# Queries and keys laid out dimensions first, and a scheduler that knows kinds of TensorE products

## The chip, the cores and the metric

The kernel runs on one core of a Trainium2 chip. The metric is the device time of one execution in microseconds (us), the median of several. TensorE (PE) multiplies, VectorE (DVE) and ScalarE (ACT) work element by element, SyncE (SP) issues most DMAs. All arithmetic that matters is in fp32 or in pairs of fp32r numbers (a high and a low part).

## The reference, cut to what matters

Attention with a feature map, then a mixture of experts, then a gated layer. Batch 4, 8 heads, 576 positions of 64 dimensions, 128 features.

```python
def phi(x):
    proj = np.einsum('bhsd,df->bhsf', x, w_phi)
    proj = proj - np.max(np.abs(proj), axis=-1, keepdims=True)
    return np.concatenate([np.exp(proj), np.exp(-proj)], axis=-1)
q_p, k_p = (phi(q), phi(k))
kv = np.einsum('bhsf,bhsd->bhfd', k_p, v)
z = np.sum(k_p, axis=2)
num = np.einsum('bhsf,bhfd->bhsd', q_p, kv)
den = np.einsum('bhsf,bhf->bhs', q_p, z)[..., None] + 1e-06
attn = num / den
# x = attn as (2304, 512): each row goes through the expert of its largest gate logit:
#   relu(x @ w1[e]) @ w2[e], times two gates; 8 experts, 1024 hidden
# then rms norm, silu(xn @ w_gate) * (xn @ w_val) @ w_out; 1536 hidden
```

## The kernel before

**Stages.** In the first stage attention and experts of the four batches are interleaved; near its end the weights of the gated layer are decoded from float64. The second stage is the gated layer in five units of rows; it has a scheduler object of its own, in which no kind of product is ever named. Between them stands a conditional for rows whose expert was guessed wrongly (L978).

**Attention, batch by batch.** A batch has nine projections: four of keys (two heads by 512 positions each), one of the leftover 64 positions of all heads, keys and queries together ("L"), four of queries. Each (`proj`, L411) takes a tile `qk` that was loaded with positions on partitions, turns it with four 128x128 transposes (L418) into a bank of the tag `pa`, copies that with ACT to `x0` (L421), and multiplies it with `w_phi` in eight products of 64 rows (L428; one half of the array for each head) into a double bank `pp`. DVE then takes the largest absolute value (L432) and subtracts it (L434), which frees `pp`. Keys: two exponentials on ACT, products with the values into half columns of the array (L492), a sum over positions on DVE (L478 to L484) that is turned by products with ones (L501), a transposition (L539). Queries: transposes (L447, recorded under L210, which calls them), two exponentials, products with 64 output partitions (L589), normalisation on DVE, transposes (L597, under L210 too), then the high part on ACT and the low part on DVE (L602) into `xh`, the experts' input.

**Experts.** `moe` multiplies in chunks of 12 matmuls of 288 columns (L737, L746), which use the whole array. It needs all of its batch's `xh`. There are two tiles `xh` and eight tiles `h` for the hidden rows, so at most two batches are under way.

**Order.** Every operation is a task with an engine, a modelled duration, a rank (`prio`; attention 100 per batch, experts from 1000) and buffers. `emit` walks through modelled time: of each engine's startable tasks it takes the one that can start first, and of those that can start when the engine comes free the one of lowest rank. The order so found is the order of instructions on each engine; on the chip an engine follows it whatever the times are. Tasks of TensorE go through `products`, which can weave tasks of kinds "load" and "pass" together. No task has the kind "load", so `products` takes one task at a time, as the other engines do. What it costs TensorE to go from whole-array products to products on half the rows or half the columns stands in the tasks' durations: 0.2 us added to each projection and to L589, 0.1 us to L492 and L501.

**Banks.** `pa` has four banks and `pp` two double ones. After a number of releases one `pp` and one `pa` go over to the experts' tag `ph` (L314, L315).

Of the kernel before, what the change touches and what calls it, by code (L numbers as in the profile page):

```python
# [41 lines left out]
class Graph:  # L42
# [4 lines left out]
    def __init__(self):  # L47
        self.free = {e: 0.0 for e in ("PE", "ACT", "DVE", "POOL", "SP")}
        self.cand = {e: [] for e in self.free}
        self.slots, self.log, self.leaving = {}, [], {}  # L50
        self.dma, self.now, self.open, self.tasks = 0.0, 0.0, 0, []
# [29 lines left out]
    def t(self, eng, dur, fn, r=(), w=(), rw=(), use=(), prio=0, nbytes=0, kind=None, steps=1, at=0.0):  # L81
        k = Task()
        k.kind, k.steps = kind, steps
        k.eng, k.dur, k.fn, k.prio, k.nbytes = eng, dur, fn, prio, nbytes
        deps = set()
        for b in r:
            deps.update(b.writers)
        for b in rw:
            deps.update(b.all)
        k.bufs = list(dict.fromkeys(list(r) + list(w) + list(rw) + list(use)))  # L90
        for b in k.bufs:
            b.all.append(k)
            b.left += 1
        for b in list(w) + list(rw):
            b.writers.append(k)
        k.n, k.succ, k.ready, k.end, k.seq = 0, [], at, None, len(self.tasks)
        for d in deps:
            if d.end is not None:
                k.ready = max(k.ready, d.end + self.lat(d.eng, eng))
            else:  # L100
                d.succ.append(k)
                k.n += 1
        self.tasks.append(k)
        self.open += 1
        if k.n == 0:
            self.cand[eng].append(k)
        return k
# [14 lines left out]
    def emit(self, until=()):  # L122
        until = list(until)
        while self.open:
            if until:
                while until and until[-1].end is not None:
                    until.pop()
                if not until:
                    break
            best = None  # L130
            for e, f in self.free.items():
                pick = None
                for k in self.cand[e]:
                    s = self.start(k)
                    if s is not None:
                        key = (max(s, f), k.prio, k.seq)
                        if pick is None or key < pick[0]:
                            pick = (key, k)
                if pick and (best is None or pick[0][0] < best[0][0]):
                    best = pick  # L140
            assert best is not None, "no task can start"
            s, k = best[0][0], best[1]
            if k.eng == "PE":
                self.products(s, k)
            else:
                self.take(k)
                k.fn()
                self.done(k, s, s + k.dur)
# [30 lines left out]
    def products(self, s, k):  # L179


        def ready(kind, wait=0.02):
            w = [(self.start(q), q) for q in self.cand["PE"] if q.kind == kind]
            return sorted((q for t, q in w if t is not None and t <= s + wait), key=lambda q: (q.prio, q.seq))

        if k.kind == "pass" and not ready("load") and ready("load", HOLD):
            rest = [q for q in ready(None) if q.prio >= 1000]
            if rest:
                k = rest[0]
        self.take(k)  # L190
        group = [k]
        n = {"load": 0, "pass": 0, k.kind: k.steps}
        while k.kind:
            short = "pass" if n["pass"] < n["load"] else "load"
            more = ready(short)
            if not more or len(group) > 1 and short == "load":
                break
            self.take(more[0])
            group.append(more[0])
            n[short] += more[0].steps  # L200
        todo = []
        for kind in ("load", "pass"):
            todo.append([(q, i + 1, f) for q in group if (q.kind or "pass") == kind
                         for i, f in enumerate(q.fn() if q.kind else [q.fn])])
        at, ends = s, []
        for i in range(max(map(len, todo))):
            for seq in todo:
                if i < len(seq):
                    q, n, f = seq[i]
                    f()  # L210
                    at += q.dur / q.steps
                    if n == q.steps:
                        ends.append((q, at))
            if i < min(map(len, todo)):
                at -= 0.05
        for q, end in ends:
            self.done(q, s, end)
        self.free["PE"] = at

# [9 lines left out]
class K:  # L229
    def __init__(self, tc, q, k, v, w_phi, wg, wo, w1, w2, mg, mv, mo, rg, out):  # L230
        self.tc, self.nc = tc, tc.nc
        self.q, self.k, self.v, self.w_phi = q, k, v, w_phi
# [69 lines left out]
    def psum(self):  # L302
# [12 lines left out]
        self.g.retire("pa", 36, one[3], "ph", lambda: one[3:])  # L315
# [35 lines left out]
    def attn_slots(self, ctx):  # L351
# [3 lines left out]
        mk("qk", 4, [P, 2, NC, D])  # L355
        mk("v", 3, [P, 2, NC, D])
        mk("vl", 2, [P, 2, NC, D])
        mk("x0", 2, [P, NC, P])
# [17 lines left out]
    def attn(self, b, prio):  # L376
# [6 lines left out]
        def load(src, pr, np_):  # L383
            t = g.buf("qk")
            if pr != "L":
                g.t("SP", 0.5, lambda: nc.sync.dma_start(
                    t.ap, src[b, 2 * pr:2 * pr + 2, 0:MAIN].rearrange("h (p c) d -> p h c d", c=NC)),
                    w=[t], prio=np_, nbytes=2 * MAIN * D * 4)
                return t
            for i, m in enumerate((self.k, self.q)):  # L390
                for j in range(2):
                    g.t(eng, 0.6, lambda i=i, j=j, m=m: dma(
                        t.ap[j * 64:(j + 1) * 64, i], m[b, j::2, MAIN:S].rearrange("h t d -> t h d")),
                        w=[t], prio=-1 if b == 0 else np_, nbytes=LEFT * H * D * 2)
# [16 lines left out]
        def proj(t, np_):  # L411

            pt, xt, m, d, pp = (g.buf(n) for n in ("pa", "x0", "m", "d", "pp"))

            def tr():
                for j in range(2):
                    for c in range(2):
                        nc.tensor.transpose(pt.ap[:, (2 * j + c) * P:(2 * j + c + 1) * P],  # L418
                                            t.ap[:, j, 2 * c:2 * c + 2].rearrange("p a d -> p (a d)"), self.ident)
            g.t("PE", 4 * 0.109, tr, r=[t], w=[pt], prio=np_)  # L420
            g.t("ACT", act(512), lambda: nc.scalar.copy(  # L421
                xt.ap.rearrange("p c t -> p (c t)"), pt.ap), r=[pt], w=[xt], prio=np_)

            def mm():
                for k in range(NC):
                    for hf in range(2):
                        r = slice(hf * 64, hf * 64 + 64)
                        nc.tensor.matmul(pp.ap[:, hf, k * FE:(k + 1) * FE], lhsT=xt.ap[r, k], rhs=self.wraw[r],  # L428
                                         start=True, stop=True)
            g.t("PE", 8 * 0.109 + 0.2, mm, r=[xt, self.cBw], w=[pp], prio=np_)  # L430
# [9 lines left out]
        at = lambda j, c: (c % 2) * NC + 2 * j + c // 2  # L440

        def queries(d, j, qp, np_):
# [3 lines left out]
            def tr():  # L446
                return [partial(nc.tensor.transpose, pd.ap[:, c * P:(c + 1) * P], d.ap[:, c % 2, 2 * j + c // 2],  # L447
                                self.ident) for c in range(NC)]
            g.t("PE", NC * 0.109, tr, r=[d], w=[pd], prio=np_, kind="pass", steps=NC)
# [20 lines left out]
        def kv_part(pr, e, v, np_, pk, part, pz=None):  # L470
# [3 lines left out]
            if es:  # L474
                ev = lambda: e.ap.rearrange("p (a k) f x -> p a k (f x)", a=2)
# [3 lines left out]
                    out=es.ap, in0=ev()[:, 0], in1=ev()[:, 1], op=ALU.add), r=[e], w=[es], prio=np_)  # L479
# [7 lines left out]
            def fn():  # L487
                for c in part:
                    for j in range(2):
                        v_, e_ = (v.ap[:, j, c], e.ap[:, at(j, c)]) if c < NC else (  # L490
# [3 lines left out]
            g.t("PE", len(part) * 0.44 + 0.1, fn, r=([e, v] if 0 in part else []) + ([el, vl] if NC in part else []),  # L494
# [9 lines left out]
            if es:  # L504
                g.t("PE", 8 * 0.06 + 0.1, zn, r=[es], rw=[pz], prio=np_)

        for i, pr in enumerate([0, "L", 1, 2, 3]):
# [4 lines left out]
            if pr == "L":  # L512
# [5 lines left out]
                queries(d, 1, qpl, np_)  # L518
# [40 lines left out]
        g.t("PE", 8 * 0.12 + 0.2, nm, r=[qpl] + list(kv.values()), w=[pn], prio=np_)  # L559
# [16 lines left out]
        for pr in range(NC):  # L576
# [4 lines left out]
            for j in range(2):  # L581
                qp = g.buf("qp")
                pn = queries(d, j, qp, np_ + j)
# [8 lines left out]
                g.t("PE", 8 * 0.12 + 0.2, nm, r=[qp, kv[pr]], rw=[pn], prio=np_ + j)  # L592
# [3 lines left out]
            def tr(px=px, x=x):  # L596
                return [partial(nc.tensor.transpose, px.ap[:, c * P:(c + 1) * P], x.ap[:, c], self.ident)  # L597
                        for c in range(NC)]
            g.t("PE", 4 * 0.109, tr, r=[x], w=[px], prio=np_ + 1, kind="pass", steps=NC)
# [434 lines left out]
HOLD = 1.0  # L1034
# [7 lines left out]
def build(tc, ctx, q, k, v, w_phi, wg, wo, w1, w2, mg, mv, mo, rg, out):  # L1042
    kk = K(tc, q, k, v, w_phi, wg, wo, w1, w2, mg, mv, mo, rg, out)
# [73 lines left out]
_INS = ["q", "k", "v", "w_phi", "moe_w_gate", "moe_w_output_gate", "moe_w1", "moe_w2",  # L1117
# [22 lines left out]
```

## Time and profile before

| | us |
|---|---|
| median of 3 runs (870.13 to 871.94) | 871.34 |
| the profiled execution | 868.49 |
| its span, first to last instruction | 866.9 |
| TensorE busy | 853.7 |
| VectorE busy | 468.3 |
| ScalarE busy | 326.4 |

The profiled execution has 1.6 us outside its span. Lines such as L418 are those of the kernel above. A timeline row merges instructions of one kind that follow each other: its first number is the start, its second the time until the last of them ends. Ends of matmuls are modelled and overlap the next start, so rates are read from start to start.

### The profile page before, as it was taken

To read this page: it belongs to the slowest core of one execution; us is meant where nothing else is said; L and a number is where in the kernel's file an instruction comes from. 1 tells how busy PE (TensorE), PEld (TensorE's weight loads), DVE (VectorE), ACT (ScalarE), POOL (GpSimd) and SP (SyncE) were. 2 spreads that over 40 slices of the span, in tenths; PEclk is the share of its full clock that TensorE was granted. 3 is DMA by queue.
4 is the path that set the end of the run, shared out by engine and by line. 5 is a ranking of instruction groups with operands and counts; after the bars stand their busy time and mean duration, and the time that the engine had idled before them with its cause. 6 is when DMAs were issued, how large, how long until landed. Compare 5 with 4: busy or idle time off the path is not lost.

```text
span 866.9 us, 15321 instructions
## 1 busy us (share of the span) xinstructions
PE 853.7 (98%) x6482; PEld 738.1 (85%) x6483; DVE 468.3 (54%) x866; ACT 326.4 (38%) x559; POOL 2.8 (0%) x17
## 2 busy tenths in 40 slices
PE   8999999999999999999999999999999999999997
PEld 6778998899889999998888889988788888888886
DVE  6987775776776489992757842431414114221111
ACT  5474453535544365550535533221214112221111
POOL 1000000000000000000000000000000000000000
PEclk9999999999999999999999999999999999999999
DMA  7354316420611656851524420020002000010001
GB/s 196 97 159 165 104 34 209 128 86 26 218 29 40 223 172 186 260 169 58 168 75 125 143 98 1 11 63 1 0 1 98 0 1 1 1 48 1 1 1 48
DMA packets 71914, 74.63 MB, mean 86 GB/s; under 512 B 13600, under 2 KB 63392, under 8 KB 71328
## 3 DMA queue, kind: packets, MB, share of 16 engines
q1 hardware_dynamic: 70592, 73.27, 26.9%
q8 instruction: 52, 0.85, 0.4%
q10 hardware_dynamic: 1248, 0.33, 0.2%
q14 instruction: 22, 0.18, 0.1%
HBM read 54.63 MB, written 18.96 MB: 85 GB/s over the span
## 4 chain that ended last, share of the span: by engine, by line
PE 52%; DVE 0%; ACT 0%; issue 0%
PE pz L925 35%; PE pz L943 17%; PE pz L896 0%; DVE yu L955 0%; ACT yu L958 0%
## 5 line engine op out<-in xcount | busy, mean ns | idle before, releaser
L925 PE MATMUL pz<-xn,wgv 128*128 128x512 f32 (+1 forms) x1200 | 258.2, 371 | 2.1 <-PEq L979 2.1
L925 PEld LDWEIGHTS pz<-xn,wgv 128*128 128x128 f32 x1200 | 210.2, 188 | 43.9 <-issue 2.3
L943 PE MATMUL pz<-wo,a 128*128 128x512 f32 x648 | 159.7, 394 | 0.0
L933 DVE TENSOR_TENSOR row<-pz,row 128x512 f32<-128x512 f32 (+1 forms) x60 | 38.2, 636 | 203.8 <-PE pz L925 200.2
L943 PEld LDWEIGHTS pz<-wo,a 128*128 128x128 f32 x648 | 121.0, 188 | 28.2 <-issue 1.4
L931 ACT ACTIVATE row<-pz 128x512 f32<-128x512 f32 (+1 forms) x60 | 33.3, 555 | 154.8 <-PE pz L925 154.6
L935 ACT CAST a<-row 128x512 fp32r<-128x512 f32 (+1 forms) x60 | 34.6, 577 | 120.5 <-DVE row L933 120.5
L737 PE MATMUL ph<-xh,w 128*128 128x288 f32 x528 | 77.6, 298 | 0.0
L737 PEld LDWEIGHTS ph<-xh,w 128*128 128x128 f32 x528 | 71.4, 188 | 0.4
L746 PE MATMUL ph<-h,w 128*128 128x288 f32 x480 | 69.5, 298 | 0.0
L746 PEld LDWEIGHTS ph<-h,w 128*128 128x128 f32 x480 | 64.7, 188 | 0.2
L432 DVE TENSOR_REDUCE m<-pq 128x8 f32<-128x1024 f32 x36 | 43.8, 1218 | 16.5 <-PE pq L428 16.5
L925 PE MATMUL pz<-xn,xh 128*128 128x512 f32 (+1 forms) x240 | 52.3, 373 | 0.0
L936 DVE TENSOR_TENSOR a<-row,a 128x512 fp32r<-128x512 f32 (+1 forms) x60 | 38.2, 637 | 25.8 <-ACT a L935 25.6
L925 PEld LDWEIGHTS pz<-xn,xh 128*128 128x128 f32 x240 | 42.1, 188 | 8.9
L767 ACT CAST w<-wr 128x1024 fp32r<-128x1024 f32 x32 | 33.5, 1048 | 31.0 <-PE ph L746 11.2
L428 PE MATMUL pq<-wraw,x 64*128 64x128 f32 x576 | 41.4, 284 | 2.9 <-DVE d L434 2.0
L768 DVE TENSOR_TENSOR w<-wr,w 128x1024 fp32r<-128x1024 f32 x32 | 39.1, 1221 | 9.6 <-ACT w L767 8.8
L434 DVE TENSOR_TENSOR d<-pq,m 128x1024 f32<-128x1024 f32 x36 | 43.7, 1217 | 0.4
L451 ACT ACTIVATE qp<-ps 128x512 f32<-128x512 f32 x64 | 34.4, 600 | 21.4 <-PE ps L210 17.6
L746 PE MATMUL ps<-h,w 128*128 128x288 f32 x288 | 41.9, 297 | 0.0
L428 PEld LDWEIGHTS pq<-wraw,x 64*128 64x128 f32 x576 | 34.9, 187 | 7.7 <-ACT x L421 2.9
(151 smaller groups left out, 934.4 us busy)
## 6 DMA issues: line engine op xcount, KB each, us to landing
wr<-in_moe_w SPq DMA_DIRECT2D x32, 512.0 KB, 4.3
xdr<-xh SPq DMA_DIRECT2D x4, 2304.0 KB, 9.0
raw<-in_moe_w_gate SPq DMA_DIRECT2D x12, 512.0 KB, 4.4
raw<-in_moe_w_val SPq DMA_DIRECT2D x12, 512.0 KB, 4.4
raw<-in_moe_w_out SPq DMA_DIRECT2D x12, 512.0 KB, 3.7
qk<-in_k SPq DMA_DIRECT2D x16, 256.0 KB, 3.4
v<-in_v SPq DMA_DIRECT2D x16, 256.0 KB, 2.8
qk<-in_q SPq DMA_DIRECT2D x16, 256.0 KB, 3.9
```

What stands on the lines that cost most here:

```text
L428: nc.tensor.matmul(pp.ap[:, hf, k * FE:(k + 1) * FE], lhsT=xt.ap[r, k], rhs=self.wraw[r], start=True, stop=True)
L432: g.t("DVE", dve(1024), lambda: nc.vector.tensor_reduce(out=m.ap, in_=pv(), axis=AX.X, op=ALU.max, apply_absolute_value=True), r=[pp], w=[ ...
L434: g.t("DVE", dve(1024), lambda: nc.vector.tensor_tensor(out=d.ap.rearrange("p h k f -> p (h k) f"), in0=pv(), in1=m.ap.unsqueeze(2).to_bro ...
L451: g.t("ACT", act(512), lambda f=f: nc.scalar.activation(qp.ap[:, f].rearrange("p c t -> p (c t)"), pd.ap, AF.Exp, scale=1.0 - 2.0 * f), r= ...
L737: self.nc.tensor.matmul(ph[:, 0:HS], lhsT=wv[:, a, c, fs], rhs=xh[:, x, c, cs], start=(c == 0 and i == 0), stop=(c == NC - 1 and i == 2))
L746: self.nc.tensor.matmul(ph[:, 0:HS], lhsT=wv[:, a, f], rhs=hs[f][:, x, cs], start=(f == 0 and i == 0), stop=(f == 7 and i == 2))
L768: g.t("DVE", dve(1024), lambda: nc.vector.tensor_tensor(out=w.ap[:, 1], in0=wr.ap, in1=w.ap[:, 0], op=ALU.subtract), r=[wr], rw=[w], prio= ...
L925: nc.tensor.matmul(ps.ap[:, 0:UT], lhsT=w[:, i, a, c], rhs=xn[c].ap[:, x, 0:UT], start=(c == 0 and n == 0), stop=(c == NC - 1 and n == 2))
L933: g.t("DVE", dve(UT), lambda sil=sil, ps=pgv[1]: nc.vector.tensor_tensor(out=sil.ap[:, 0:UT], in0=ps.ap[:, 0:UT], in1=sil.ap[:, 0:UT], op= ...
L935: g.t("ACT", act(UT, False), lambda sil=sil, a=a: nc.scalar.copy(a.ap[:, 0, 0:UT], sil.ap[:, 0:UT]), r=[sil], w=[a], prio=pr)
L936: g.t("DVE", dve(UT), lambda sil=sil, a=a: nc.vector.tensor_tensor(out=a.ap[:, 1, 0:UT], in0=sil.ap[:, 0:UT], in1=a.ap[:, 0, 0:UT], op=ALU ...
L943: nc.tensor.matmul(po[t].ap, lhsT=a.ap[:, x, ts], rhs=w[:, y], start=(f == 0 and n == 0), stop=(f == NF - 1 and n == 2))
```

## The change

Three things are edited together.

1. The host lays `q` and `k` out anew: for two heads, 128 rows (head, dimension) of 512 positions. The leftover positions of both go into a new input `l` of the same form. `proj` multiplies straight from the loaded tile: the four transposes, the bank and the ACT copy are gone. A load is 128 rows of 2 KB; the leftovers of a batch are one DMA in place of four. `qk` has six buffers in place of four, and `x0` (two buffers) is gone.
2. `products` is gone; TensorE's tasks are taken like those of other engines. Projections have the kind "rows"; L492, L501, L556 and L589 the kind "cols"; the others have none. Among TensorE's tasks that can start equally early, those of the kind of the task before count 1.5 ranks lower. A task whose kind differs from the one before is modelled 0.2 us longer; the fixed 0.1 and 0.2 us are out of the durations.
3. The tile `e` is indexed by head and position block in order, so the operands of the sum L478 are two pieces of 512 numbers instead of one of 1024. The bank that leaves `pa` does so after 22 releases in place of 36.

```diff
-                        key = (max(s, f), k.prio, k.seq)
+                        key = (max(s, f), k.prio - (1.5 if e == "PE" and k.kind == self.kind else 0), k.seq)
...
-            if k.eng == "PE":
-                self.products(s, k)
-            else:
-                self.take(k)
-                k.fn()
-                self.done(k, s, s + k.dur)
+            self.take(k)
+            k.fn()
+            dur = k.dur
+            if k.eng == "PE" and k.kind != self.kind:
+                self.kind, dur = k.kind, k.dur + 0.2
+            self.done(k, s, s + dur)
...
-        self.g.retire("pa", 36, one[3], "ph", lambda: one[3:])
+        self.g.retire("pa", 22, one[3], "ph", lambda: one[3:])
...
-        mk("qk", 4, [P, 2, NC, D])
+        mk("qk", 6, [P, NC, P])
-        mk("x0", 2, [P, NC, P])
...
-                    t.ap, src[b, 2 * pr:2 * pr + 2, 0:MAIN].rearrange("h (p c) d -> p h c d", c=NC)),
+                g.t("SP", 0.5, lambda: nc.sync.dma_start(t.ap, src[b, pr].rearrange("p (c t) -> p c t", c=NC)),
...
+                g.t(eng, 0.6, lambda: dma(t.ap, self.l[b].rearrange("p (c t) -> p c t", c=NC)),
...
-            g.t("PE", 4 * 0.109, tr, r=[t], w=[pt], prio=np_)
-            g.t("ACT", act(512), lambda: nc.scalar.copy(
-                xt.ap.rearrange("p c t -> p (c t)"), pt.ap), r=[pt], w=[xt], prio=np_)
...
-                        nc.tensor.matmul(pp.ap[:, hf, k * FE:(k + 1) * FE], lhsT=xt.ap[r, k], rhs=self.wraw[r],
+                        nc.tensor.matmul(pp.ap[:, hf, k * FE:(k + 1) * FE], lhsT=t.ap[r, k], rhs=self.wraw[r],
...
-            g.t("PE", 8 * 0.109 + 0.2, mm, r=[xt, self.cBw], w=[pp], prio=np_)
+            g.t("PE", 8 * 0.109, mm, r=[t, self.cBw], w=[pp], prio=np_, kind="rows")
...
+    for n in "qk":
+        a = inputs[n][:, :, :MAIN].reshape(B, NC, 2, P, NC, D)
+        lay[n] = a.transpose(0, 1, 2, 5, 4, 3).reshape(B, NC, P, MAIN)
+    a = np.stack([inputs[n][:, :, MAIN:].reshape(B, 2, 2, 2, LEFT, D) for n in "kq"])
+    lay["l"] = a.transpose(1, 3, 6, 0, 2, 4, 5).reshape(B, P, MAIN)
```

## Rows read from the trace of the kernel before

**Rows 1.** The page: busy time, share of the span, instructions; 40 slices in tenths.

```profile
PE 853.7 (98%) x6482; PEld 738.1 (85%) x6483; DVE 468.3 (54%) x866; ACT 326.4 (38%) x559; POOL 2.8 (0%) x17
...
PE   8999999999999999999999999999999999999997
...
PEclk9999999999999999999999999999999999999999
```

**Rows 2.** Busy time of the engines by stretch, with granted clock and DMA.

```profile
0.00:8.00 8.00, 5.79 (x44) 5.57 (x47) 0.01 (x1) 2.46 (x5) 2.77 (x17) 1.00 0.66 179
8.00:63.80 55.80, 51.73 (x755) 41.66 (x754) 52.42 (x94) 33.88 (x57) 0.00 (x0) 1.00 0.49 140
63.80:183.40 119.60, 119.60 (x1341) 106.13 (x1339) 86.06 (x179) 55.88 (x102) 0.00 (x0) 1.00 0.41 129
183.40:302.40 119.00, 119.00 (x1479) 107.90 (x1479) 82.40 (x191) 53.82 (x98) 0.00 (x0) 1.00 0.30 102
302.40:409.30 106.90, 104.30 (x778) 102.92 (x778) 83.96 (x145) 52.81 (x90) 0.00 (x0) 1.00 0.57 174
409.30:866.90 457.60, 453.23 (x2096) 373.92 (x2096) 163.49 (x257) 127.55 (x211) 0.00 (x0) 1.00 0.13 42
```

**Rows 3.** DVE's groups from 8 to 63.8 us: count, busy, mean ns, idle before.

```profile
L432 DVE TENSOR_REDUCE m<-pq 128x8 f32<-128x1024 f32 x12 | 14.5, 1214 | 8.1 <-PE pq L428 8.1
L434 DVE TENSOR_TENSOR d<-pq,m 128x1024 f32<-128x1024 f32 x11 | 13.2, 1210 | 0.0
L478 DVE TENSOR_TENSOR es<-e 128x1024 f32<-128x1024 f32 x5 | 6.1, 1214 | 0.0
```

**Rows 4.** The transposes L418 alone, by stretch: busy PE, busy weight loads.

```profile
0.00:8.00 8.00, 1.04 (x8) 1.02 (x8) 1.00 0.66 179
8.00:63.80 55.80, 7.95 (x55) 5.94 (x56) 1.00 0.49 140
63.80:302.40 238.60, 12.12 (x83) 8.92 (x81) 1.00 0.35 115
```

**Rows 5.** TensorE's timeline, around 95 us and around 308 us.

```profile
93.87 1.87 PE L737 MATMUL ps<-xh,w 128*128 128x288 f32 x12
95.58 0.60 PE L418 MATMUL ps<-ident,qk 128*128 128x128 f32 x4
95.94 1.83 PE L737 MATMUL ph<-xh,w 128*128 128x288 f32 x12
97.70 1.16 PE L428 MATMUL pq<-wraw,x 64*128 64x128 f32 x16
...
308.15 3.34 PE L737 MATMUL ph<-xh,w 128*128 128x288 f32 x24
311.33 1.75 PE L737 MATMUL ps<-xh,w 128*128 128x288 f32 x12
```

**Rows 6.** TensorE's timeline of the first 14 us.

```profile
4.87 1.04 PE L418 MATMUL ps<-ident,qk 128*128 128x128 f32 x8
6.83 2.06 PE L428 MATMUL pq<-wraw,x 64*128 64x128 f32 x32 [0.92 <-ACT x L421]
8.99 1.09 PE L418 MATMUL ps<-ident,qk 128*128 128x128 f32 x8
11.67 2.20 PE L428 MATMUL pq<-wraw,x 64*128 64x128 f32 x32 [1.58 <-DVE d L434]
```

**Rows 7.** TensorE's timeline: first chunk after transposes, then before column products; last switch.

```profile
78.55 1.85 PE L737 MATMUL ps<-xh,w 128*128 128x288 f32 x12
80.23 1.74 PE L737 MATMUL ph<-xh,w 128*128 128x288 f32 x12
...
101.63 1.82 PE L737 MATMUL ps<-xh,w 128*128 128x288 f32 x12
103.38 1.15 PE L556 MATMUL ps<-kv,qpl 128*64 128x65 f32 x32
104.37 1.10 PE L589 MATMUL ps<-kv,qp 128*64 128x65 f32 x32
105.40 1.16 PE L428 MATMUL pq<-wraw,x 64*128 64x128 f32 x16
...
284.41 2.09 PE L589 MATMUL ps<-kv,qp 128*64 128x65 f32 x64
286.42 3.42 PE L746 MATMUL ps<-h,w 128*128 128x288 f32 x24
```

**Rows 8.** The end of the first stage: DVE's last decoding, TensorE's first product after.

```profile
388.56 0.69 DVE L840 TENSOR_TENSOR xh<-row,xh 128x512 fp32r<-128x512 f32 x1
...
409.30 11.13 PE L925 MATMUL pz<-xn,wgv 128*128 128x512 f32 x48 [2.09 <-PEq L979]
```

## What the change is predicted to do

> **What bounds the kernel now.** I read the page first. TensorE is busy for 98% of the span, at full granted clock in all 40 slices [rows 1]. Such an average says that TensorE's work sets the end; it doesn't say that each microsecond taken from TensorE comes off the time. So I cut the span into stretches [rows 2]. The reader is to compare the TensorE column (first) with the VectorE column (third) in each:
>
> - 8 to 63.8 us, before the first expert product: VectorE is busy 52.4 of 55.8 us, TensorE 51.7. Both are full, but VectorE is fuller. From here on only it can say when batch 0 is done.
> - 63.8 to 302.4 us: TensorE is busy 119.6 of 119.6 and 119.0 of 119.0 us, VectorE 86 and 82. Expert chunks fill every gap that attention leaves. This is bound by TensorE alone.
> - 302.4 to 409.3 us: experts and decoding. TensorE is idle for 2.6 us, of which 2.1 are the conditional. VectorE's last decoding ends at 389 us, 20 us before TensorE's next stage starts [rows 8].
> - From 409.3 us: the second stage. The change touches nothing in it, so its 457.6 us stay.
>
> The question for each edit is therefore in which of the first two stretches it lies.
>
> **The transposes.** L418 has 144 matmuls in 36 groups of four. By stretch they are 8 + 55 + 83, and as the cut at 63.8 falls into a group that began at 63.4, 64 of them (16 groups) stand before the first expert product and 80 (20 groups) behind it [rows 4]. What a group costs where TensorE is full: an expert chunk of 12 takes 1.59 us if the next chunk follows (24 in 3.18 us, from 308.15 to 311.33); with a group between, it is 2.07 us from the chunk at 93.87 to the one at 95.94 [rows 5]. So 0.48 us here. The chunk behind a group starts slowly wherever one stands (1.68 us from 78.55 to 80.23, [rows 7]), and another transposition often stands next to it and would leave that tail in place, so I take 0.45 us. Twenty groups: **-9.0 us** (0.36 us each, the group's own start to start from 95.58 to 95.94, would give -7.2; 0.48 gives -9.6).
>
> The other sixteen groups lie under VectorE. Freed time there is worth something only if VectorE gets its work sooner. Two such places are seen.
>
> - The start. TensorE transposes at 4.87 and can multiply only at 6.83, after the ACT copy [rows 6]; VectorE begins 1.2 us later. Without the two steps the first projection runs at 4.87, so VectorE's full stretch starts **2.0 us** sooner. I know of nothing that takes this back: the first load, which started the transposes at 4.87, is the same 256 KB in longer rows.
> - VectorE's idle time in the stretch is 55.8 - 52.4 = 3.4 us. A TensorE with less to do can close part of it. Bounds 0 and 3.4; I take **1 us**, since most of it is waits at the end of batch 0, where ACT and TensorE follow each other.
>
> Together -3.0 us. The first expert chunk would come at about 60.8 us in place of 63.8. It can't come much sooner without leaving work of batch 1 undone that is done before it now, and that work then stands behind it on a full TensorE: no gain.
>
> In the same stretch TensorE will be seen idle for longer: the 16 groups at 0.45 us are 7.2 us less work in a stretch only 1 us shorter behind its start. That is the part of the gain that is lost, and the reader should not look for 36 x 0.45 = 16 us.
>
> **The ACT copies.** They are gone with the transposes. ACT is busy 34 of 55.8 us and less than half of the later stretches [rows 2], so apart from the start they are worth nothing in themselves. If that cover failed, ACT would still only have less to do.
>
> **Loads.** The same bytes in fewer DMAs; DMA is busy 0.30 to 0.49 in the stretches that hold attention behind the start [rows 2]. Loads are issued further ahead with six buffers, while a buffer is now held until the projection instead of the transposition. Cost nothing; bound from the first row of that view, where DMA is busiest (0.66): if a load came late there, TensorE would wait as it does now before the third and fourth projection, 1.58 us [rows 6], and VectorE with it. Bounds 0 and +1.6.
>
> **The sum with two pieces.** L478 reads two runs of 512 instead of one of 1024. It takes 1.21 us; L434, whose second operand is repeated along each row, takes 1.21 us too [rows 3], so the shape of the operand shows no price. I take 0; were each 0.1 us longer, five in VectorE's stretch make +0.5.
>
> **The kinds.** What a switch costs: a chunk that follows transposes takes 1.68 us when a chunk is next and 1.75 us when column products are next; column products take 0.99 us before more of them and 1.03 us before row products [rows 7]. From start to start of single instructions I count the same more exactly: the last expert matmul before such products takes 0.09 us more than one within, and the last column product about 0.10 us more. I take 0.09 us. Counted over the timeline there are 157 switches among whole, rows and columns, the first behind 4.87 us [rows 6], the last at 286.42 [rows 7], 119 of them behind 63.8 us. All that grouping could ever give is therefore 119 x 0.09 = 10.7 us, and most can't be had. The new rule only chooses among attention tasks within 1.5 ranks that are ready together; expert chunks have ranks from 1000, so it never keeps TensorE on them, and a burst of attention products between two chunks has two switches at the least. I find about 50 bursts behind 63.8 us that hold such products, so some 100 switches must stay if bursts don't merge. I take 12 saved: **-1.1 us** (bounds 0 and, if bursts merge down to half the switches, -5.4).
>
> The Trainium skill says the same in a rule of its own: "TensorEngine Tiling (Array Packing)", Key Properties, says that changing the tiling mode, not merely the tile, drains TensorE. It gives no price; by the rule alone one would expect a scheduler that groups kinds to gain on all 157.
>
> **The plan's own model.** Each switch is now modelled at 0.2 us, back to whole-array products too, where the trace shows about 0.09. TensorE will be ahead of the plan by up to 157 x 0.11 = 17 us over the stage. An engine ahead of its plan waits at the next task whose inputs aren't there. I take 0: behind 63.8 us VectorE has 28% idle time and TensorE shows no wait at all [rows 2], and an expert chunk stands before nearly every burst. The bound is the whole 17 us.
>
> **Sum.** -9.0 - 3.0 - 1.1 = -13.1 us; the profiled execution of 868.49 us would be 855.4, and the median 871.34, which lies 2.85 us above it, **858 us**.
>
> **The rivals.**
>
> *The start doesn't move* (0.17). TensorE's new order favours column products over the next projection, VectorE waits for it, and the first chunk is again at 63.8. For it: VectorE has next to no slack there. Against: `pp` lets two projections stand ready. -9.0 - 1.1 gives 861; with the dearer bounds (7.2 and a late load) 865.
>
> *Bursts merge* (0.12). With 36 fewer tasks and the rule, attention's products gather; half of the switches go, and the batch-0 stretch closes all of VectorE's idle time: -9.6 - 5.4 - 5.4 = -20.4, 851; with work moved out of the first stretch somewhat lower. Against: the bursts are made by when tasks come ready, which the rule leaves alone.
>
> *The plan is partly wrong* (0.09). A third to half of the 17 us becomes waits of TensorE: 864 to 867.
>
> *Slower: TensorE waits in its fixed order* (0.03). All 17 us become waits: 858 + 17 = 875. It decides from 13 us of waits on. It would be seen as TensorE idle behind 63.8 us, where it is 0 now.
>
> *Slower: the clock falls* (0.02). After the first two projections, at about 7 us, TensorE must wait for VectorE to free `pp`: two maxima and a subtraction of 1.21 us, less the overlap, so until about 9.7. That is a longer pause than the 1.58 us of now [rows 6]. If the granted clock fell to the 1.2 GHz level and stayed there through the stretch, its work of 51.7 - 7.2 = 44.5 us would take 89, and TensorE would bound the stretch in VectorE's place: 858 + 36 = 894. It decides when the low clock covers more than some 8 us of that work. Against: the clock is 1.00 in each stretch, beside pauses of 0.92 and 1.58 us. The skill's "TensorE: Matmul & The Clock Gate", in the section on HAM oscillation, warns of idle gaps between bursts, and this speaks against the change; the trace so far shows no such fall.
>
> *No difference* (0.02): the waits just eat the gain.
>
> **Chances and range.** The forecast has 0.55, its own range 853 to 862 (sum with -7.2 and no switches saved, to -9.6, 2 us more of VectorE's idle time and 25 fewer switches). To leave out no more than 2 in 10 the range reaches into the merged bursts below and over the partly wrong plan above: **849 to 867 us**. Faster by over 0.2% (1.7 us, about what a measurement of this kernel can tell): 0.93; within: 0.02; slower: 0.05.
>
> **What would show it.** Right: L418 and L421 gone; VectorE's first L432 near 6.1 us; the first L737 between 59 and 62; TensorE idle 5 us or more between 8 us and that chunk, and not at all from there to the conditional; 135 to 150 switches; the stage's end near 396; the second stage within 1 us of 457.6. Wrong: waits of TensorE behind the first chunk (the plan), a first chunk at 63 or later (the start), under 110 switches (merged bursts), a granted clock below 1.00 (the clock), or a VectorE sum longer than 1.21 us.

## The result, and the profile after

The changed kernel takes 857.43 us (median of 4 runs, 857.07 to 858.34) where the kernel before took 870.74 beside it (869.95 to 871.94): a ratio of 0.9848, with a 95% interval of 0.9831 to 0.9865. A second measurement, on another occasion, gave 858.68 us and 0.9870 (0.9849 to 0.9891). 858 was forecast. The profiled execution took 858.34 us, with a span of 856.7, against 868.49 and 866.9.

The views that answer to [rows 2] are read first: busy time by stretch of the changed kernel, cut where its own stages begin (TensorE, its weight loads, VectorE, ScalarE, GpSimd, granted clock, DMA share, GB/s). The last line is from TensorE's timeline.

```profile
0.00:8.00 8.00, 5.78 (x48) 5.48 (x49) 1.80 (x3) 1.50 (x3) 2.77 (x17) 1.00 0.71 210
8.00:64.50 56.50, 50.57 (x739) 40.10 (x739) 52.35 (x97) 30.66 (x50) 0.00 (x0) 0.97 0.50 153
64.50:180.00 115.50, 115.50 (x1389) 101.65 (x1388) 91.59 (x199) 49.34 (x88) 0.00 (x0) 1.00 0.39 125
180.00:295.00 115.00, 115.00 (x1318) 103.05 (x1318) 76.13 (x176) 47.59 (x86) 0.00 (x0) 1.00 0.34 119
295.00:398.20 103.20, 100.73 (x754) 99.80 (x753) 81.32 (x138) 51.08 (x86) 0.00 (x0) 1.00 0.53 163
398.20:856.70 458.50, 453.50 (x2096) 373.80 (x2096) 163.71 (x257) 127.45 (x211) 0.00 (x0) 1.00 0.13 42
...
410.53 2.80 PE L886 MATMUL pz<-wo,a 128*128 128x512 f32 x11 [0.93 <-DVE wo L783]
```

Three things are to be seen. The second stage is within a microsecond of what it was (458.5 against 457.6 us; TensorE has one new wait in it, 0.93 us for VectorE's weights `wo` ahead of 410.53 us). Between the first expert chunk and the second stage TensorE is as full as before, and that part has shrunk from 345.5 us (63.8 to 409.3) to 333.7 (64.5 to 398.2). The part ahead of the first chunk has not shrunk at all: 64.5 against 63.8. In it TensorE now idles for 56.5 - 50.6 = 5.9 us behind 8 us, where it was 4.1.

The start of the first chunk does not tell the whole gain, though. TensorE's timeline of the changed kernel shows what stands ahead of it (L541 turns the last part of the experts' input of batch 0, L591 to L597 and L605 are the gate, L444 and L482 are products with ones and a transposition of batch 1, L373 its projections, L680 is the first chunk):

```profile
56.82 0.63 PE L444 MATMUL ps<-ones,es 128*64 128x1 f32 x16
57.38 1.16 PE L373 MATMUL pq<-wraw,qk 64*128 64x128 f32 x16
58.48 0.44 PE L482 MATMUL ps<-ident,ks 128*128 128x128 f32 x2
58.75 0.60 PE L541 MATMUL ps<-ident,x 128*128 128x128 f32 x4
59.11 0.37 PE L591 MATMUL ps<-xh,wgt 128*32 128x288 f32 x1
...
61.43 0.30 PE L597 MATMUL ps<-xh,wgt 128*16 128x288 f32 x1 [1.08 <-DVE xh L545]
...
62.73 1.16 PE L373 MATMUL pq<-wraw,qk 64*128 64x128 f32 x16
63.93 0.66 PE L605 MATMUL ps<-ident,lgT 32*128 32x32 f32 x5
64.52 1.73 PE L680 MATMUL ph<-xh,w 128*128 128x288 f32 x11
```

All 16 gate products have come ahead of the first chunk; before, the gate came after two chunks. Counted over the timelines of both kernels, these stand ahead of the first chunk now and stood behind it before, with their time from start to start in these rows: the gate's 16 products (2.1 us at 0.13 each), the five small transposes L605 (0.6), one projection (1.1), 16 products with ones (0.6) and two transposes L482 (0.3). Together this is about 4.6 us of work. What says when batch 0 is done is VectorE's last low part. Its row and that of VectorE's first largest value, in the timeline of the kernel before and then of the changed one:

```profile
8.04 2.35 DVE L432 TENSOR_REDUCE m<-pq 128x8 f32<-128x1024 f32 x2 [7.93 <-PE pq L428]
...
62.67 0.69 DVE L602 TENSOR_TENSOR xh<-ps,xh 128x512 fp32r<-128x512 f32 x1
```

```profile
6.22 2.36 DVE L377 TENSOR_REDUCE m<-pq 128x8 f32<-128x1024 f32 x2 [6.11 <-PE pq L373]
...
60.69 0.68 DVE L545 TENSOR_TENSOR xh<-ps,xh 128x512 fp32r<-128x512 f32 x1
```

Batch 0 is done 2.0 us sooner, and VectorE's full stretch began 1.8 us sooner.

The groups of VectorE that answer to [rows 3], from 6 to 64.5 us, show no new price for the sum with two pieces (L421, 1217 ns against 1214):

```profile
L377 DVE TENSOR_REDUCE m<-pq 128x8 f32<-128x1024 f32 x13 | 15.8, 1219 | 9.6 <-PE pq L373 9.4
L379 DVE TENSOR_TENSOR d<-pq,m 128x1024 f32<-128x1024 f32 x12 | 14.5, 1216 | 0.1
L421 DVE TENSOR_TENSOR es<-e 128x1024 f32<-128x1024 f32 x5 | 6.1, 1217 | 0.0
```

The clock is new. TensorE pauses for 2.69 us ahead of the third projection, where it was 1.58 [rows 6], and for about 0.5 us at several places up to 31 us. Then, in the windows of the changed kernel from 30 us, and in the timelines of TensorE and VectorE:

```profile
9.76 2.29 PE L373 MATMUL pq<-wraw,qk 64*128 64x128 f32 x32 [2.69 <-DVE d L379]
...
30.00:32.00 2.00, 1.48 (x22) 1.08 (x22) 1.94 (x4) 0.60 (x2) 0.00 (x0) 1.00 0.54 153
32.00:35.40 3.40, 3.40 (x27) 2.83 (x26) 2.50 (x6) 2.08 (x5) 0.00 (x0) 0.51 0.00 0
35.40:38.00 2.60, 2.60 (x82) 2.40 (x83) 2.60 (x5) 0.00 (x0) 0.00 (x0) 0.99 0.32 107
...
33.15 2.08 PE L373 MATMUL pq<-wraw,qk 64*128 64x128 f32 x16
35.16 0.56 PE L482 MATMUL ps<-ident,ks 128*128 128x128 f32 x2
35.27 1.22 DVE L377 TENSOR_REDUCE m<-pq 128x8 f32<-128x1024 f32 x1 [0.90 <-PE pq L373]
```

The clock is at its lower level of 1.2 GHz for 3.4 us, and one projection in it takes 2.0 us from start to start (33.15 to 35.16) where others take 1.09. VectorE waits 0.90 us for it.

### The profile page after: what moved, and what is told of

Its sections match the earlier page's. It is cut to its first block, busy times and chain, and to the rows that moved or that the text cites. A ratio compares the mean times of both kernels' runs of the same rounds, so it can differ in the third digit from the quotient of the medians.

```text
span 856.7 us, 14958 instructions
## 1 busy us (share of the span) xinstructions
PE 841.1 (98%) x6338; PEld 723.9 (84%) x6339; DVE 466.9 (54%) x866; ACT 307.6 (36%) x523; POOL 2.8 (0%) x17
## 4 chain that ended last, share of the span: by engine, by line
PE 52%; DMA 1%; DVE 0%; issue 0%; ACT 0%; DVEq 0%; SPq 0%
PE pz L868 34%; PE pz L886 17%; DMA raw<-in_moe_w_out 1%; PE pz L839 0%; DVE row L773 0%; DVE a L879 0%; DVE row L779 0%; DVE wo L783 0%; DVE yu L898 0%; ACT yu L901 0%; DVE row L876 0%; DVEq L879 0%; DVE row L776 0%; DVEq L773 0%; SPq L770 0%
## 5 line engine op out<-in xcount | busy, mean ns | idle before, releaser
L680 PE MATMUL ph<-xh,w 128*128 128x288 f32 x528 | 77.5, 299 | 0.7 <-DVE h L729 0.7
L680 PEld LDWEIGHTS ph<-xh,w 128*128 128x128 f32 x528 | 71.5, 188 | 3.0 <-issue 1.2
L373 PE MATMUL pq<-wraw,qk 64*128 64x128 f32 x576 | 42.8, 289 | 4.0 <-DVE d L379 4.0
L373 PEld LDWEIGHTS pq<-wraw,qk 64*128 64x128 f32 x576 | 36.0, 191 | 9.1 <-DVE d L379 5.4
```

What stands on the lines that cost most here:

```text
L373: nc.tensor.matmul(pp.ap[:, hf, k * FE:(k + 1) * FE], lhsT=t.ap[r, k], rhs=self.wraw[r], start=True, stop=True)
L680: self.nc.tensor.matmul(ph[:, 0:HS], lhsT=wv[:, a, c, fs], rhs=xh[:, x, c, cs], start=(c == 0 and i == 0), stop=(c == NC - 1 and i == 2))
```

## The experiments

The theory is that of the prediction: VectorE sets the pace until batch 0 is done, TensorE alone behind it, so a transposition saves its 0.45 us behind the first chunk only; grouping kinds is worth little. The rivals: each microsecond of TensorE counts everywhere; the scheduler carries a good part of the gain.

**Layout and scheduler apart.** `layout_only` takes the new rule and price out again:

```diff
-                        key = (max(s, f), k.prio - (1.5 if e == "PE" and k.kind == self.kind else 0), k.seq)
+                        key = (max(s, f), k.prio, k.seq)
-                self.kind, dur = k.kind, k.dur + 0.2
+                self.kind = k.kind
...
-            g.t("PE", 8 * 0.109, mm, r=[t, self.cBw], w=[pp], prio=np_, kind="rows")
+            g.t("PE", 8 * 0.109 + 0.2, mm, r=[t, self.cBw], w=[pp], prio=np_, kind="rows")
```

The column products get their 0.1 and 0.2 us back in the same way.

> The new layout without the kinds: no preference, no modelled price of a switch, the fixed 0.1 and 0.2 us back in the durations, everything else as in the changed kernel. Theory (the gain is the 36 groups of transposes, as far as TensorE sets the pace; grouping is worth about 1 us or nothing, since the changed kernel has 162 switches against 157): 856 to 859 us, against 870.7 before. Rival (half of the gain comes from the scheduler): 863 to 865 us.

Measured: 860.28 us (857.83 to 860.46), ratio 0.9881 (0.9863 to 0.9898). The layout alone gives 10 of the 13 us, 1.3 us above the 856 to 859 that were expected. Its interval overlaps that of the changed kernel, and its profile shows 162 switches, the same number (switches are counted in the timeline up to the second stage, by whether a product uses the whole array, half its rows or half its columns; the gate's smallest products count as whole). Its executions had a mean granted clock of 0.993 to 0.997, the changed kernel's 0.995 to 0.998, and at 0.995 both were measured: 857.83 and 859.67 against 859.95 us. So the missing 3 us are not shown to be the scheduler's.

`kinds_only` puts the rule, the kinds and the price on the old layout:

> The kinds, the preference and the modelled 0.2 us on the old layout, transposes and copies as before. Theory: 869 to 872 us, no difference, with 145 to 165 switches. Rival (half of the gain comes from the scheduler): 863 to 865 us. Second rival (the plan charges a switch too dearly and TensorE runs into waits): 873 us or more, with idle time of TensorE behind the first expert chunk.

Measured: 870.89 us (869.28 to 874.79), ratio 1.0008 (0.9994 to 1.0021), 167 switches, TensorE idle for 2.5 us behind the first chunk, where it was 2.6. No difference: neither a gain from the kinds nor the waits that the second rival feared. The switches are two more than expected.

`pref0` keeps the price and drops the preference; `cost009` keeps the preference and lowers the price:

```diff
-                        key = (max(s, f), k.prio - (1.5 if e == "PE" and k.kind == self.kind else 0), k.seq)
+                        key = (max(s, f), k.prio, k.seq)
...
-                self.kind, dur = k.kind, k.dur + 0.2
+                self.kind, dur = k.kind, k.dur + 0.09
```

> The changed kernel without the preference of 1.5 ranks, a switch still modelled at 0.2 us. Theory (the bursts are made by when tasks come ready): 157 to 170 switches, within 1.5 us of 857.4. Rival (the preference saves switches that would be there without it): over 175 switches and +1.5 us or more.

> The changed kernel with a switch modelled at 0.09 us in place of 0.2, near what the trace shows. Theory (the model's price moves the order a little and nothing waits behind the first chunk either way): within 2 us of 857.4. Rival (the dear price makes TensorE outrun its plan): 2 to 5 us faster.

Measured: `pref0` 858.42 us, ratio 0.9856 (0.9840 to 0.9871), 158 switches; `cost009` 858.95 us, ratio 0.9865 (0.9848 to 0.9883), 158 switches. With the preference it was 162. The preference saves no switch and no time that these runs can tell.

**TensorE's work put back.** `tr123` and `tr0` write four transposes into the projection's bank just ahead of its products; `more` is `b > 0` in the first and `b == 0` in the second (such a projection is also modelled at 12 products in place of 8):

```diff
             def mm():
+                if more:
+                    for k in range(NC):
+                        nc.tensor.transpose(pp.ap[:, 0, k * FE:(k + 1) * FE], t.ap[:, k], self.ident)
```

> The changed kernel with the same four transposes put back into each of the 27 projections of batches 1 to 3. Four of these projections stand ahead of the first expert chunk. Theory (behind it TensorE alone sets the pace): 23 x 0.45 = +10.4 us, 866 to 869.5. Rival (another engine or the chain of attention sets the pace there too): under +5 us.

Measured: 870.59 us (868.37 to 873.01), ratio 1.0006 (0.9994 to 1.0018). Putting back 27 of 36 groups eats the whole gain. The windows, and the last rows ahead of the first chunk in its timeline:

```profile
8.00:68.90 60.90, 55.17 (x775) 43.24 (x775) 54.72 (x101) 31.23 (x50) 0.00 (x0) 0.97 0.54 166
68.90:410.20 341.30, 338.79 (x3530) 312.73 (x3528) 247.06 (x508) 146.69 (x259) 0.00 (x0) 1.00 0.40 127
...
66.64 1.95 PE L440 MATMUL ps<-e,v 128*64 128x256 f32 x16
68.42 0.60 PE L440 MATMUL ps<-el,vl 128*64 128x256 f32 x4
68.95 3.31 PE L685 MATMUL ph<-xh,w 128*128 128x288 f32 x23
```

Behind the first chunk it is 341.3 us against 333.7, +7.6. But the 20 products of the last rows, 2.3 us from start to start, stand ahead of the chunk here and behind it in the changed kernel. So the 23 groups cost 7.6 + 2.3 = 9.9 us, or 0.43 us each. The chunk came 4.4 us later, 2.3 of it for these products. The span is 12.4 us longer, 2 more than the theory had: the other 2.1 us lie ahead of the chunk, where the four early groups stand, which it took to be free. VectorE was done with batch 0 1.5 us later there.

> The changed kernel with four transposes put back into each of the nine projections of batch 0, as idle work of TensorE into the projection's own bank; no copy, no result read. Theory (VectorE sets the pace until batch 0 is done): the first projection ends 0.44 us later and the rest is hidden, +0.4 to +1.2 us over the changed kernel's 857.4. Rival (every microsecond of TensorE counts wherever it stands): 9 x 0.45 = +4.0 us. With the granted clock at 1.00 throughout if the busier TensorE keeps it up, which would give back up to 1.5 us.

Measured: 860.94 us (859.34 to 861.54), ratio 0.9894 (0.9878 to 0.9911). That is 2.3 us over the second measurement of the changed kernel and 3.5 over the first, nearer to the rival. Its mean clock (0.995 to 1.000) was no lower, so the clock doesn't explain it. The timeline of TensorE in `tr0` shows how it differs from the kernel before, where transposes ran ahead into banks of their own:

```profile
4.87 1.06 PE L374 MATMUL pq<-ident,qk 128*128 128x128 f32 x4
5.86 1.57 PE L378 MATMUL pq<-wraw,qk 64*128 64x128 f32 x16
...
11.57 0.66 PE L374 MATMUL pq<-ident,qk 128*128 128x128 f32 x4 [2.46 <-DVE d L384]
12.16 1.16 PE L378 MATMUL pq<-wraw,qk 64*128 64x128 f32 x16
```

Each group now stands between VectorE's release of the bank (the wait of 2.46 us) and the projection that VectorE needs next, so it lengthens VectorE's own loop. The first group also stood first of all, and VectorE began at 7.47 us in place of 6.22. This says little, as the start differs from profile to profile without any edit there. TensorE's first two projections in the changed kernel, in its second measurement and in `cost009`, with VectorE's first row at 6.22, 6.78 and 7.35 us:

```profile
4.90 2.17 PE L373 MATMUL pq<-wraw,qk 64*128 64x128 f32 x32
...
5.01 2.63 PE L373 MATMUL pq<-wraw,qk 64*128 64x128 f32 x32
...
5.01 3.20 PE L373 MATMUL pq<-wraw,qk 64*128 64x128 f32 x32
```

Behind the first chunk `tr0` shows no change (334.2 us). So the theory had to say not only in which stretch work lies, but whether it lies in the loop of the engine that sets the pace. `tr0_bank` tests that, with the same work ahead of the loop:

```diff
+            if b == 0:
+                pt = g.buf("pa")
+
+                def tr():
+                    for k in range(NC):
+                        nc.tensor.transpose(pt.ap[:, k * P:(k + 1) * P], t.ap[:, k], self.ident)
+                g.t("PE", 4 * 0.109, tr, r=[t], w=[pt], prio=np_)
...
-        self.g.retire("pa", 22, one[3], "ph", lambda: one[3:])
+        self.g.retire("pa", 31, one[3], "ph", lambda: one[3:])
```

> The nine groups of transposes of batch 0 are back again, but as tasks of their own into a bank of pa, ahead of the projection as in the kernel before, and not between the release of pp and the projection as in tr0; no copy, nobody reads them. Theory (in the first stretch only what stands in VectorE's loop costs; tr0 was dear because its transposes lay in that loop and ahead of the first projection at the low clock): within 1.5 us of the control, with idle time of TensorE 2 to 4 us less before the first chunk. Rival (each microsecond of TensorE costs there too): +4 us over the control.

> The changed kernel once more, unedited, as the control for the three beside it: 856.5 to 859 us, with a mean granted clock of 0.995 to 0.998, and the shorter times at the higher clock.

Measured beside each other: the control 858.68 us (857.63 to 859.95), `tr0_bank` 857.19 us (856.63 to 859.26), ratios 0.9870 and 0.9860 (0.9837 to 0.9882). Nine groups of transposes in batch 0 show no price here, where the rival had 4 us. The windows of `tr0_bank`:

```profile
8.00:64.40 56.40, 53.08 (x774) 41.95 (x770) 53.45 (x98) 30.44 (x50) 0.00 (x0) 1.00 0.52 155
64.40:398.20 333.80, 331.21 (x3456) 304.51 (x3456) 248.94 (x511) 147.58 (x260) 0.00 (x0) 1.00 0.42 135
```

TensorE's idle time ahead of the chunk went from 5.9 to 3.3 us, and the chunk and the stage's end stand where they stood. The clock has a part in this: it is 1.00 ahead of the chunk here and 0.97 in the changed kernel's profile, and the means were 0.997 to 1.000 against 0.995 to 0.998. Of the kernel before, the executions at 0.997 took 1.7 us more than those at 1.000 (870.3 and 868.5 on average). By that, the changed kernel's 858.0 at 0.997 would be an estimated 856.3 at 1.000, where `tr0_bank` took 856.63 and 857.16: at equal clock the nine groups cost some 0.6 us by this estimate.

The loop shows in a comparison that the clock does not disturb, `tr0` against `tr0_bank`: in both profiles it is 1.00 in the whole stage. VectorE's first largest value and last low part of batch 0, in `tr0` and then in `tr0_bank`:

```profile
7.47 1.23 DVE L382 TENSOR_REDUCE m<-pq 128x8 f32<-128x1024 f32 x1 [7.35 <-PE pq L378]
...
62.47 0.68 DVE L550 TENSOR_TENSOR xh<-ps,xh 128x512 fp32r<-128x512 f32 x1
...
7.42 2.36 DVE L384 TENSOR_REDUCE m<-pq 128x8 f32<-128x1024 f32 x2 [7.30 <-PE pq L380]
...
60.55 0.68 DVE L552 TENSOR_TENSOR xh<-ps,xh 128x512 fp32r<-128x512 f32 x1
```

They begin together, and `tr0` is done with batch 0 1.9 us later. The spans differ by 2.3 us (857.8 and 855.5), the medians by 3.8. The same work is dear inside the loop and nearly free ahead of it.

**VectorE's work doubled.** `max0` and `max123` take the largest value twice, in batch 0 and, with `b > 0` in the condition, in the others:

```diff
+            if b == 0:
+                g.t("DVE", dve(1024), lambda: nc.vector.tensor_reduce(
+                    out=m.ap, in_=pv(), axis=AX.X, op=ALU.max, apply_absolute_value=True), r=[pp], rw=[m], prio=np_)
```

> The changed kernel with VectorE's largest value taken twice in the nine projections of batch 0: nine more instructions of 1.13 us from start to start, +10.2 us of VectorE. Theory (VectorE sets the pace until batch 0 is done): the first expert chunk comes 8 to 10 us later; TensorE has more time for batch 1 in between, but that needs VectorE too: +6 to +10 us. Rival (TensorE sets the pace there too): under +3 us.

Measured: 865.74 us (863.27 to 866.99), ratio 0.9940 (0.9924 to 0.9956), +7 to +8 us. Its windows, and the row and the windows of the start, where TensorE pauses for 4.95 us:

```profile
8.00:76.10 68.10, 55.25 (x754) 43.34 (x755) 65.35 (x111) 30.75 (x49) 0.00 (x0) 0.90 0.40 114
76.10:405.70 329.60, 327.10 (x3442) 303.35 (x3441) 244.80 (x507) 146.75 (x260) 0.00 (x0) 1.00 0.43 139
```

```profile
12.93 3.78 PE L373 MATMUL pq<-wraw,qk 64*128 64x128 f32 x32 [4.95 <-DVE d L382]
...
7.00:10.20 3.20, 0.99 (x17) 0.80 (x15) 3.07 (x3) 0.00 (x0) 0.00 (x0) 1.00 0.99 329
10.20:17.00 6.80, 4.07 (x34) 3.78 (x36) 5.75 (x6) 3.90 (x4) 0.00 (x0) 0.50 0.49 131
```

The first chunk comes 11.6 us later, and the part behind it is 4.1 us shorter, as 20 products of batch 1 (2.3 us, the same as in `tr123`) have come ahead of it and 15 switches have gone. VectorE is busy for 65.35 of the 68.10 us, so it does set the pace there. The clock falls to the lower level at 10.2 us, inside the long pause, stays there for 6.8 us and is there again for 6.8 us in two later stretches ahead of the chunk; that is part of the price.

> The same for the 27 projections of batches 1 to 3: +30.5 us of VectorE, of which some 4 instructions ahead of the first chunk. Theory (VectorE has room there: busy 91.6 of 115.5 and 76.1 of 115.0 us): +2 to +6 us, from the four early ones and a few waits. Rival (VectorE is a bound there too): +15 us or more.

Measured: 866.42 us (860.86 to 869.74), ratio 0.9954 (0.9935 to 0.9973), +8 to +9 us: more than forecast, far less than the rival's 15. The windows:

```profile
61.20:69.30 8.10, 7.08 (x55) 4.84 (x55) 5.21 (x8) 2.18 (x5) 0.00 (x0) 0.58 0.98 365
69.30:404.70 335.40, 333.25 (x3477) 305.97 (x3474) 276.10 (x538) 149.05 (x264) 0.00 (x0) 1.00 0.42 131
```

Behind the first chunk VectorE works 27.1 us more (276.1 against 249.0) and the part is 1.7 us longer (335.4 against 333.7). So VectorE has room there, as the theory says; of the 1.7 us, 1.1 are a projection that stands ahead of the chunk in the changed kernel. The price lies ahead: the chunk comes 4.8 us later. Only three of the added instructions stand there, VectorE began 1.1 us later in this profile (7.31 us), and the clock is low from 61.2 us on, with TensorE waiting 2.09 us for VectorE just before. The means of the granted clock were 0.986 to 0.996, lower than the changed kernel's, and the execution at 0.996 took 860.86 us, inside what was forecast.

**Keeping the clock.** `fill_f24b` and `fill_c24` add 24 idle products, the second with the price of 0.09 us too:

```diff
-        self.g.retire("pa", 22, one[3], "ph", lambda: one[3:])
+        self.g.retire("pa", 46, one[3], "ph", lambda: one[3:])
...
+        for i in range(n):
+            w = self.g.buf("pa")
+            self.g.t("PE", 0.214, lambda w=w: self.nc.tensor.matmul(
+                w.ap[:, 0:P], lhsT=self.mean, rhs=self.mean, start=True, stop=True), w=[w], prio=450, at=t0 + dt * i)
...
+        kk.fill(24, 5.5, 0.9)
```

> The changed kernel with 24 idle products of 128 columns (about 0.21 us each) of a rank behind all attention and ahead of the experts, startable from 5.5 us on, one each 0.9 us; each takes a free bank and nobody reads it. They fill pauses of TensorE in the stretch that VectorE sets. Theory (the pauses let the granted clock fall, and the low clock lengthens the projections that VectorE waits for): the clock of that stretch is 1.00 in more of the runs, mean clock 0.998 or more, 0.5 to 2 us faster than the control. Rival (the low clock there is hidden behind VectorE): the same time, or slower by what the products delay.

> The same 24 idle products with a switch modelled at 0.09 us. Theory: the clock as with the idle products alone, the time within 1.5 us of that kernel. Rival (the plan's price matters once the clock is steady): over 2 us faster than it.

Measured beside the control of 858.68 us: `fill_f24b` 858.70 (856.41 to 859.25), ratio 0.9864 (0.9841 to 0.9887), mean clock 0.998 to 1.000; `fill_c24` 859.32 (858.85 to 860.55), ratio 0.9883 (0.9864 to 0.9902), mean clock 0.998 to 0.999. The clock is higher and the median no lower. So the gain of 0.5 to 2 us did not come. In the profile of `fill_f24b` the first stretch is at 1.00, but the clock falls where the second stage begins:

```profile
8.00:63.80 55.80, 54.19 (x783) 44.06 (x782) 52.53 (x97) 30.17 (x49) 0.00 (x0) 1.00 0.49 148
63.80:398.20 334.40, 331.61 (x3462) 304.87 (x3461) 249.57 (x511) 148.30 (x261) 0.00 (x0) 1.00 0.42 136
398.20:402.70 4.50, 4.48 (x13) 3.56 (x14) 0.00 (x0) 0.00 (x0) 0.00 (x0) 0.62 0.32 73
```

No version that was run is shown to be faster than the changed kernel.

## Why the prediction was right, point by point

**The transposes behind the first chunk, -9.0.** Right in the mechanism and somewhat too large. The part shrank by 11.8 us, of which 4.6 us of work only moved ahead: 11.8 - 4.6 = 7.2, or 7.7 if the added switches (below) are set against it. For twenty groups this is 0.36 to 0.39 us each. `tr123` puts 23 groups back behind the chunk and they cost 9.9 us, 0.43 each. Forecast were 0.45 us, with bounds of 0.36 and 0.48.

**The sixteen groups under VectorE, nothing of their own.** Right for the nine of batch 0, within the clock's share: `tr0_bank` has them back ahead of the loop, and the time is no longer (an estimated 0.6 us at equal clock). `tr0` adds the condition: inside the loop they cost about 2 us more. The four groups of batch 1 that stood ahead of the chunk were only put back inside the loop (`tr123`).

**The start, -2.0, and VectorE's idle time, -1.** VectorE began 1.8 us sooner in the profile, and batch 0 was done 2.0 us sooner. Such a start is not sure: in `layout_only` VectorE began at 8.18 us, as late as before, and in most other profiles of the new layout between 6.6 and 7.5. The 1 us from closing VectorE's idle time did not come. The mark that was named, the first chunk between 59 and 62 us, was wrong: 64.5, since the order put more work ahead of it. The prediction said that an earlier chunk leaves work undone; here the opposite happened, TensorE's spare time took up 4.6 us of work that stood behind the chunk. Ahead of the chunk the profile thus gains 4.6 - 0.7 = 3.9 us, in another form than forecast.

**The kinds, -1.1.** The step that failed. There are 162 switches and not 135 to 150, and 125 of them behind the first chunk where it was 119, so the term is 6 x 0.09 = +0.5 us if anything. `kinds_only` and `pref0` show no gain from the rule. The rule of the Trainium skill, "TensorEngine Tiling (Array Packing)", Key Properties, that a change of tiling mode drains TensorE, agrees with the 0.09 us of a switch that the prediction reads from the trace. That the array drains, no run here shows. The likely reason why nothing was saved is the one that the prediction had against its own term: attention's products come ready a few at a time and expert chunks stand between, so there is hardly anything to group. That `pref0` has no more switches without the preference fits this; the reason itself was not tested.

**The plan's own model, 0.** Right: behind the first chunk TensorE idles for 2.5 us in all, as before, and `cost009` makes no difference.

**The rivals.** Merged bursts and a TensorE that waits in its order are excluded by the rows above, and the start did move in the profiled execution. The clock did fall, against the forecast's clock of 1.00, but for 3.4 us and not for the stretch: one projection 0.9 us longer, and VectorE waited 0.9 us behind it. The pause that the rival named came as worked out (until 9.76 us), and the clock stayed at 1.00 for 22 us behind it.

**The sum.** -13.1 was forecast and the medians differ by 13.3 (and 11.4 in the second measurement). The two profiled executions differ by 10.2 only: -7.2 behind the chunk, -3.9 ahead of it and +0.9 in the second stage; their mean clocks were 0.999 and 0.997. Of the kernel before, 14 executions at a mean clock of 0.997 took 870.3 us on average; of the changed one, 5 at the same clock took 858.0. At equal clock the gain is 12.3 us, so the sum was about 1 us too large. That it came so near is partly luck: behind the chunk the profiles show 7.2 us where 9.0 + 1.1 were forecast, and more than the forecast 3.0 ahead of it.

**What stays open.** Whether anything but the clock lies in the 1.6 to 2.9 us between `layout_only` and the changed kernel: the intervals overlap, its clocks were lower, and in its profile VectorE began late and the clock fell at another place. Why the first two projections take longer in some executions than in others, no run shows. The ACT copies and the longer rows of the loads were not put back apart from the transposes.

## What to carry to other kernels

Cut the span where another engine takes over the pace, and pay for removed work only where its engine is full. In the other stretches ask whether the work lies inside the loop of the engine that sets the pace: the same nine groups of transposes cost about 2 us more inside VectorE's loop than ahead of it. When a part is cut at an event such as the first chunk, count which work has crossed the cut before reading a price from the part's length. Grouping instructions by kind needs a queue of ready work; count the switches that the order leaves before expecting them to go.

## What the runs showed of the hardware

Most of the spread between executions of the kernel before goes with TensorE's granted clock. From its 46 results beside the experiments:

| mean granted clock | executions | us, lowest to highest |
|---|---|---|
| 1.000 | 4 | 868.31 to 868.77 |
| 0.999 | 10 | 868.37 to 869.06 |
| 0.998 | 5 | 869.71 to 870.25 |
| 0.997 | 14 | 869.91 to 871.08 |
| 0.996 | 2 | 871.34 to 871.43 |
| 0.995 | 11 | 871.38 to 871.69 |

The changed kernel follows the same line more loosely, from 857.07 to 859.09 at 0.997 or 0.998 to 859.95 at 0.995. In the profiles the clock fell at three places: at the start, where TensorE pauses for 2.5 to 4.95 us (`max0`, `cost009`, `pref0`); at some time between 27 and 62 us, with shorter pauses before it (the changed kernel, at 32.0 us, `tr123`, `max0`, `max123`, `pref0`); and where the second stage begins, behind the 1.8 to 2.3 us of the conditional. That last pause is of this length in every profile, yet the clock fell there in `layout_only`, `fill_f24b`, `tr123`, `max0`, `max123` and `pref0` and not in the other profiles, the changed kernel's among them. The Trainium skill, "TensorE: Matmul & The Clock Gate", in the section on HAM oscillation, says that idle gaps between bursts throttle TensorE again; the rows of `max0` from inside the pause of 4.95 us on agree. Why the same pause is punished in one execution and not in the next, no run here shows.
